# A hand-ordered attention and soft-MoE kernel: the last 64 rows' scores in float32r, two transfers fewer a pair of heads, four shared PSUM banks, and a new order of all operations

## The chip, the cores and the metric

The kernel runs on one core of a Trainium2 chip. The metric is the device time of one execution in microseconds (us); lower is better. Three executions of the kernel before took 482.61, 485.45 and 488.31 us, so its median is 485.45 us. The execution whose profile is read below took 482.46 us.

## The reference

Attention over 8 batches, 8 heads, 576 positions and head width 64, in float32, mixed with a read from a memory matrix; the result is rearranged to 4608 tokens of width 512 and goes through a soft mixture of 8 experts with 4 slots each.

```python
scores = scale * np.matmul(q, k.transpose(0, 1, 3, 2))
causal = np.triu(np.ones((S, S), dtype=bool), k=1)
scores = np.where(causal, -1000000000.0, scores)
...
local = np.matmul(a, v)
q_p = phi(q)
mem_ret = np.einsum('bhsd,bhde->bhse', q_p, M_prev)
mem_norm = np.einsum('bhsd,bhd->bhs', q_p, z_prev)[..., None] + 1e-06
...
return (g * mem_out + (1 - g) * local).astype(np.float32)
...
logits = x @ phi
...
slot_input = d.T @ x
...
    h = np.maximum(slot_input[e] @ w1[e], 0.0)
    slot_out[e] = h @ w2[e]
...
return (c @ slot_out).astype(np.float32)
```

## The kernel before

The 64 (batch, head) problems are handled as 32 pairs of heads, `n` = 0 to 31; the two heads of a pair share the 128 partitions. Each pair goes through the same list of small operations, each a Python function `op_<name>` of a few instructions:

- **Loads**, all issued by SyncE's queue (SP): `loadq` (L380, both the transposed q and three 128-column blocks in which the two heads' 64 rows stand block-diagonally), `loadk` (L385), `loadv` (L390, two transfers, one for each half of the partitions, into one buffer `vt` that all pairs share) and `loadm` (L395, memory matrix and norm).
- **Scores.** The 576 query rows are cut into rows 128 to 511 (`s.q1`, `s.q2`, `s.q3`) and the ends: rows 0 to 63 (`s.a`), 64 to 127 (`s.b`) and 512 to 575 (`s.z` for keys 0 to 511, `s.zb` for the last 64). `s.q*` multiplies in float32r (L437): q and k are split into a rounded high part and a remainder, `X[:, 0]`, `X[:, 1]` (by `qhi`, L359/L357, and `qlo`, L404) and `K2[:, 0]`, `K2[:, 1]` (by `kn`, `kl`, L410), and three products of the parts are added up, each over 64 partitions for each head. The ends go through `quads` (L415): float32 products in four column groups of 32. A float32 product of this kind stands in the trace as two instructions.
- **Softmax.** `max.*` on VectorE (DVE, L466) masks, scales, leaves PSUM and finds the maximum; `exp.*` on ScalarE (ACT, L474); `t.*` transposes the probabilities on TensorE (PE, L564) and `te.*` (ACT L354 or DVE L357) takes them out of PSUM.
- **Output.** `av.*` and `memb` (L415) multiply by v; `mema` (L415) multiplies the feature map of q by the memory. Two rows of factors travel through DRAM to be broadcast over partitions: the memory's norm (`nrw` L544 writes it, `nrr` L550 reads it back into `rb`, and `qn` L554 multiplies `qp` by it ahead of `mema`) and the softmax sums (`rt`, `rte`, then `rrw` L495 to L497 writes them in four transfers, `rrr` L501 reads them back into `rr`, and `xe.0` L635 and `mo` L628 multiply by them).
- **The soft MoE's statistics** (`x1` to `x5`) run over each finished block of 512 tokens, between the pairs' operations; after the last pair comes a closing part (`y*`), and then the experts (L934, L951) and the combination (L1008).

The order is written out by hand. `SEQ` lists 2546 operations such as `t.2@0:1` (operation, pair, and after the colon the PSUM bank); the operations are emitted in that order and `pin()` keeps every engine's instructions in it, the queue of SP's transfers too. A second table, `EV`, says for each movable operation which engine does it: `a` ACT, `v` DVE, `p` POOL (GpSimd). The weights of the experts are loaded meanwhile by 44 operations `w@x` in the same list (512 KB each).

PSUM's banks are three of `psT`, used in turn by transposes, norms, memory products and the MoE's pieces; one of `psO` for the running output `oa`; and two double ones of `psS` for scores.

Of the kernel before, what the change touches and what calls it, by code (L numbers as in the profile page):

```python
# [51 lines left out]
t.4@0:1 exp.q3h1@1 neps@1 rrw@0 max.q3h0@1 t.3@0:2 nmk@1 exp.q2h0@1 t.5@0:0 max.q2h1@1 exp.q3h0@1 s.q1@1:1 te.5@0 w@1
s.z@1 kn@2 exp.q2h1@1 max.zb@1 nred@1 te.3@0 te.4@0 t.0@1:0 nrw@1 exp.a@1 qhi@2 t.1@1:2 loadq@3 exp.b@1 max.q1h1@1
kl@2 t.2@1:1 max.z@1 exp.q1h1@1 av.0@0 rrr@0 qn@0 exp.z@1 max.q1h0@1 s.a@2:0 s.zb@2 av.2@0 max.zb@2 exp.q1h0@1 te.0@1
av.1@0 te.2@1 nrr@1 max.a@2 qlo@2 av.6@0 mema@0:10 te.1@1 loadk@3 rec@1 memb@0 av.3@0 qmin@2 loadm@2 s.b@2 loadv@1
rt@1:2 max.b@2 rte@1 s.q1@2:1 rrw@1 s.q2@2 max.q1h1@2 qexp@2 xe.0@0 s.z@2 mo@0 exp.a@2 exp.q1h1@2 xe.1@0 t.3@1:2
t.4@1:0 max.q2h0@2 te.3@1 x3.0@0:1 max.q2h1@2 te.4@1 t.5@1:2 qphi@2 x3e.0@0 s.q3@2:0 te.5@1 max.z@2 rrr@1 norm@2:0
kn@3 qn@1 av.0@1 exp.z@2 qhi@3 neps@2 exp.q2h1@2 mema@1:21 max.q1h0@2 qlo@3 nmk@2 exp.b@2 nred@2 exp.q1h0@2 s.b@3:1
kl@3 loadm@3 s.a@3 max.q3h1@2 av.3@1 exp.q2h0@2 nrw@2 av.6@1 memb@1 s.zb@3 max.q3h0@2 av.1@1 loadk@4 qmin@3 loadq@4
max.b@3 exp.q3h0@2 max.a@3 s.q2@3 exp.q3h1@2 s.q3@3:0 max.q2h1@3 qexp@3 xe.0@1 t.1@2:0 rec@2 nrr@2 t.3@2:1 te.1@2  # L60
max.q2h0@3 av.2@1 te.3@2 qphi@3 exp.q2h1@3 rt@2:0 loadv@2 t.5@2:1 max.zb@3 max.q3h1@3 rte@2 exp.q2h0@3 s.q1@3:1 rrw@2
max.q3h0@3 norm@3:0 te.5@2 max.q1h0@3 s.z@3 exp.q3h1@3 mo@1 s.zb@4:0 s.a@4 w@2 exp.q3h0@3 neps@3 t.4@2:1 xe.1@1 nmk@3
t.0@2:0 qhi@4 te.4@2 max.q1h1@3 x3.1@0:2 max.zb@4 qlo@4 te.0@2 max.a@4 nred@3 t.2@2:1 kn@4 t.0@3:0 x3e.1@0 nrw@3
exp.a@4 s.b@4 rrr@2 te.2@2 qn@2 av.0@2 exp.b@3 max.z@3 exp.a@3 mema@2:12 loadq@5 exp.q1h1@3 kl@4 exp.q1h0@3 av.3@2
qmin@4 loadm@4 exp.z@3 memb@2 av.6@2 loadk@5 s.q2@4 te.0@3 nrr@3 rec@3 s.q1@4:1 max.q2h1@4 rt@3:0 max.q2h0@4 av.2@2
rte@3 qexp@4 rrw@3 max.b@4 av.1@2 exp.b@4 exp.q2h1@4 xe.0@2 s.q3@4:0 mo@2 loadv@3 t.4@3:0 xe.1@2 qhi@5 t.3@3:2 te.4@3
max.q3h0@4 t.1@3:1 te.3@3 kn@5 max.q3h1@4 t.5@3:0 te.1@3 t.2@3:2 qphi@4 te.5@3 rrr@3 s.z@4 qn@3 te.2@3 exp.q3h1@4
norm@4:1 max.q1h1@4 s.zb@5:0 mema@3:20 neps@4 exp.q3h0@4 qlo@5 nmk@4 max.q1h0@4 kl@5 s.a@5 s.b@5 loadm@5 qmin@5
max.z@4 av.0@3 loadk@6 qexp@5 max.a@5 av.6@3 av.2@3 exp.z@4 qphi@5 memb@3 av.3@3 exp.q2h0@4 nred@4 av.1@3 exp.q1h0@4
max.b@5 nrw@4 exp.q1h1@4 loadq@6 mo@3 s.q3@5:1 loadv@4 xe.1@3 s.q2@5 w@3 norm@5:1 xe.0@3 x1.0@0:2 rec@4 neps@5  # L70
max.q3h1@5 x1.1@0 nmk@5 rt@4:0 x1l@0 nrr@4 t.3@4:1 max.q2h1@5 rte@4 t.0@4:2 max.q2h0@5 te.3@4 t.5@4:0 max.zb@5 exp.a@5
max.q3h0@5 rrw@4 t.4@4:1 te.0@4 x1m@0 te.5@4 s.q1@5:0 s.z@5 te.4@4 qhi@6 max.q1h1@5 kn@6 qlo@6 s.b@6:1 nred@5 x1e@0
loadk@7 av.0@4 max.z@5 nrw@5 kl@6 exp.q3h1@5 t.2@4:2 max.q1h0@5 t.1@4:0 te.2@4 x2@0:1 rrr@4 qn@4 exp.z@5 s.q3@6:0
x2m@0 exp.q1h1@5 s.q2@6 x2a@0 exp.q2h0@5 te.1@4 memb@4:2 mema@4:1 nrr@5 exp.q3h0@5 max.q3h0@6 exp.b@5 av.3@4 max.b@6
av.2@4 exp.q1h0@5 max.q3h1@6 loadm@6 loadq@7 s.zb@6 exp.q2h1@5 av.6@4 av.1@4 max.zb@6 max.q2h0@6 x2e@0 qmin@6 rec@5
s.z@6:0 loadv@5 qexp@6 xe.0@4 exp.q3h1@6 t.2@5:0 mo@4 t.4@5:2 te.2@5 xe.1@4 s.q1@6 te.4@5 qphi@6 rt@5:0 t.3@5:1 rte@5
# [1037 lines left out]
```

## Time and profile before

| | |
|---|---|
| runs of the kernel before | 482.61, 485.45, 488.31 us |
| profiled execution | 482.46 us, of which span 480.7 us |
| attention, 12 to 400 us of the span | PE 372.54 us busy of 388.00 |
| after 400 us (closing part, experts, combination) | 80.7 us |

The profile is read by engine: an engine is busy when an instruction runs on it, its idle time is put down to what ended it, and lines as L415 are those of the listing above. A helper's line stands for several operations: L415 is every float32 product in column groups, L437 every float32r score, L564 the transposes of probabilities. "PEld" is the loading of the stationary operand, which can run beside a product. All transfers of the pairs are issued on one queue, SP's, and run on 16 DMA engines.

### The profile page before, as it was taken

Reading aid. Unit: us, or ns where it says so; the run is one execution under the profiler, and the core shown is the slowest. Engines: PE = TensorE matmul, PEld = TensorE weight load, DVE = VectorE, ACT = ScalarE, POOL = GpSimd, SP = SyncE. Lnnn points to the kernel's source line nnn. Section 1 sums busy time; section 2 is a strip of 40 time slices with the busy share of each in tenths; the row PEclk is TensorE's granted clock in tenths of the full one; section 3 lists DMA queues with packets and bytes.
Section 4 is the critical chain, followed back from the end, with each engine's and each line's share of the span. In section 5 each row is a group of like instructions: output and inputs, shape, how many; then the busy total and the mean of one; then the engine's idle time right before and its main releaser. Section 6 shows DMA issues by size and latency. Waiting matters only on the chain.

```text
span 480.7 us, 16135 instructions
## 1 busy us (share of the span) xinstructions
PE 445.5 (93%) x6082; PEld 280.2 (58%) x6082; DVE 371.6 (77%) x1301; ACT 349.2 (73%) x1007; POOL 122.2 (25%) x139
## 2 busy tenths in 40 slices
...
GB/s 218 213 145 170 192 187 192 136 208 135 212 196 141 176 217 215 216 226 180 199 227 203 175 139 161 161 181 188 191 215 189 222 213 326 298 415 408 134 338 334
DMA packets 66300, 102.03 MB, mean 212 GB/s; under 512 B 11248, under 2 KB 41520, under 8 KB 66224
## 3 DMA queue, kind: packets, MB, share of 16 engines
...
## 4 chain that ended last, share of the span: by engine, by line
PE 46%; DMA 25%; DVE 15%; ACT 5%; SPq 4%; issue 3%; POOL 0%; DVEq 0%; ACTq 0%; POOLq 0%
PE oa L415 9%; DMA rm<-rs 9%; PE psT L564 8%; DMA rb<-rd 6%; PE psS L415 6%; DMA qq<-in_q_dram 5%; PE psS L437 5%; PE psT L415 4%; PE pf L934 3%; PE pc L1008 3%; DVE q L466 3%; DMA w<-in_w_dram 3%; DVE zq L466 2%; ACT w L354 2%; PE pf L951 2%
## 5 line engine op out<-in xcount | busy, mean ns | idle before, releaser
L354 ACT COPY at<-psT 128x512 f32<-128x512 f32 (+1 forms) x210 | 90.7, 481 | 30.8 <-PE psT L564 23.9
L474 ACT ACTIVATE q<-q,nm 128x384 f32<-128x384 f32 (+2 forms) x160 | 97.6, 613 | 5.5 <-DVE nm L466 5.4
L415 PE MATMUL oa<-at,mv 128*32 128x448 f32 (+4 forms) x1280 | 99.3, 423 | 1.1 <-DMA mv<-in_v_dram 1.0
L466 DVE CUSTOM_DVE_ANT_0 q<-psS,mv 128x512 f32<-128x512 f32 (+1 forms) x128 | 76.5, 613 | 6.2 <-PE psS L437 4.9
L564 PE MATMUL psT<-cs,q 128*128 128x128 f32 x480 | 74.0, 280 | 5.4 <-DVE xt L636 2.4
L474 ACT ACTIVATE zq<-zq,nm 128x256 f32<-128x256 f32 (+2 forms) x128 | 67.9, 533 | 8.7 <-DVE nm L466 8.5
L437 PE MATMUL psS<-K,X 64*128 64x512 f32 (+2 forms) x576 | 68.1, 358 | 1.6 <-DVE nm L466 1.6
L564 PEld LDWEIGHTS psT<-cs,q 128*128 128x128 f32 x480 | 53.9, 141 | 21.3 <-issue 5.8
L415 PE MATMUL psS<-k,qq 128*32 128x64 f32 (+2 forms) x1280 | 59.9, 298 | 1.3 <-DVE nm L466 1.2
L437 PEld LDWEIGHTS psS<-K,X 64*128 64x128 f32 x576 | 44.9, 184 | 17.0 <-issue 8.4
L564 PE MATMUL psT<-cs,zq 128*128 128x128 f32 x288 | 47.4, 278 | 2.3 <-DVE xt L636 0.9
L415 PEld LDWEIGHTS oa<-at,mv 128*32 128x32 f32 x1280 | 34.2, 110 | 25.1 <-issue 15.2
L415 PEld LDWEIGHTS psS<-k,qq 128*32 128x32 f32 x1280 | 33.4, 110 | 25.7 <-issue 9.6
L509 POOL TENSOR_SCALAR qp<-qq 128x576 f32<-128x576 f32 x15 | 24.9, 1658 | 61.5 <-PE psT L415 48.4
L415 PE MATMUL psT<-qp,q 128*32 128x64 f32 (+1 forms) x512 | 37.2, 407 | 2.3 <-DVE qp L554 1.8
L410 POOL TENSOR_TENSOR K<-k,K 128x512 fp32r<-128x512 f32 x28 | 36.9, 1317 | 7.1 <-ACT K L354 6.6
L564 PEld LDWEIGHTS psT<-cs,zq 128*128 128x128 f32 x288 | 32.9, 141 | 7.7 <-issue 1.5
L466 DVE CUSTOM_DVE_ANT_0 zq<-psS,mv 128x256 f32<-128x256 f32 x64 | 26.4, 419 | 12.4 <-PE psS L415 10.5
L415 PEld LDWEIGHTS psT<-qp,q 128*32 128x32 f32 x512 | 15.4, 109 | 27.3 <-issue 20.4
L474 ACT ACTIVATION_READ_ACCUMULATOR q<-q,nm 128x1 f32 x160 | 31.0, 194 | 0.0
L404 POOL TENSOR_TENSOR X<-qq,X 128x384 fp32r<-128x384 f32 x24 | 25.0, 1043 | 22.1 <-DVE X L357 12.2
L534 POOL TENSOR_TENSOR rn<-rn,rm 128x144 f32<-128x144 f32 x22 | 10.8, 491 | 75.4 <-DVE rn L529 35.8
...
## 6 DMA issues: line engine op xcount, KB each, us to landing
...
```

Source lines behind the costliest of these rows:

```text
L354: nc.scalar.copy(o, i)
L404: ALU_ENG[ev("qlo", n)].tensor_tensor(out=X[:, 1, 0:384], in0=st[n]["q"][:, 128:512], in1=X[:, 0, 0:384].bitcast(F32), op=ALU.subtract)
L410: ALU_ENG[ev("kl", n)].tensor_tensor(out=K2[:, 1, :], in0=st[n]["k"][:, 0:512], in1=K2[:, 0, :].bitcast(F32), op=ALU.subtract)
L415: nc.tensor.matmul(o[32 * g:32 * g + 32], w[:, 32 * g:32 * g + 32], x(g), start=start, stop=stop)
L437: nc.tensor.matmul(ps[:, c0:c0 + N], X[ROW[h], x, 128 * i - 128:128 * i], K2[ROW[h], y, 0:N], start=(x, y) == (0, 0), stop=(x, y) == (0, 1))
L466: nc.vector.tensor_tensor_reduce(out=sm, in0=src, in1=msk, op0=ALU.add, op1=ALU.min, scale=-0.125, scalar=m0, accum_out=acc_o)
L474: nc.scalar.activation(sm, sm, AF.Exp, scale=-1.0, bias=s["nm"][:, J:J + 1], accum_out=s["sum"][:, J:J + 1])
L509: ALU_ENG[ev("qmin", n)].tensor_scalar(out=st[n]["qp"], in0=st[n]["q"], scalar1=0.0, scalar2=None, op0=ALU.min)
L534: ALU_ENG[ev("nmk", n)].tensor_tensor(out=rn, in0=rn, in1=maskn.rearrange("a (u o) -> a u o", o=1).broadcast_to([128, 16, 9]), op=ALU.mult)
L564: nc.tensor.transpose(out=ps[:, 128 * x:128 * x + 128], in_=src[:, k0:k0 + 128], identity=ident)
L934: nc.tensor.matmul(ps[32 * g:32 * g + 32, :], si[:, c, 32 * (4 * eg + g):32 * (4 * eg + g) + 32], wt[0, eg, f, c // 2, g][:, c % 2, :], st ...
L1008: nc.tensor.matmul(ps[:, v2], (cst4[u][0:96, t4, :] if t4 < 8 else cst8[0:96, u, :]), so[0:96, dh], start=True, stop=True)
```

## The change

1. **`s.z` in float32r.** The block-diagonal copy of rows 512 to 575 now stands in `X` too, behind rows 128 to 511, and `s.z` becomes three products over the full 128 by 128 array for each of its two stretches of 256 keys (six instructions), where there were four column groups, twice two instructions each (sixteen). `X` grows from 384 used columns to 576, and so `qhi` and `qlo`. `s.zb` stays.
2. **Transfers.** `loadv` becomes one transfer of 128 partitions by 768 numbers (384 KB), with its zeros in it; it was two of 64 by 640 (160 KB each), and two memsets at the start. `rrw` writes its first six rows in one transfer, not two. A pair issues twelve transfers instead of fourteen.
3. **PSUM.** `psO` goes, and `oa` takes its bank from `psT`, which has four now.
4. **`qn`** may now run on POOL: in `EV` 23 pairs do it there and 9 on DVE; all 32 did it on DVE.
5. **The order.** `SEQ`, `EV` and `WORD` (which buffers late weights take) are written anew throughout.

```diff
-EV.update(qphi="v", qn="v")
+EV.update(qphi="v")
...
-        nc.gpsimd.memset(vt[64:128, 0], 0.0)
-        nc.gpsimd.memset(vt[0:64, 5], 0.0)
...
-    psO = tc.alloc_tile_pool(name="psO", bufs=1, space=PSUM)
...
-    X = spl.tile([128, 2, 512], F32R, name="X")
+    X = spl.tile([128, 2, S], F32R, name="X")
...
     def op_loadq(n):
         b, p = divmod(n, NP)
-        st[n]["q"] = qq[:, n % 2, 384:]
-        st[n]["qd"] = qq[:, n % 2, 0:384].rearrange("a (i x) -> a i x", i=3)
+        t = qq[:, n % 2]
+        st[n]["q"], st[n]["qx"], st[n]["qd"] = t[:, 256:832], t[:, 384:960], (t[:, 0:128], t[:, 128:256], t[:, 832:960])
...
     def op_loadv(n):
         b, p = divmod(n, NP)
-        for h in range(2):
-            nc.sync.dma_start(out=vt[ROW[h], h:h + 5], in_=v[b, p, ROW[h]])
+        nc.sync.dma_start(out=vt, in_=v[b, p])
...
     def op_qhi(n):
-        ENG[ev("qhi", n)](X[:, 0, 0:384], st[n]["q"][:, 128:512])
+        ENG[ev("qhi", n)](X[:, 0], st[n]["qx"])
 
     def op_qlo(n):
-        ALU_ENG[ev("qlo", n)].tensor_tensor(out=X[:, 1, 0:384], in0=st[n]["q"][:, 128:512], in1=X[:, 0, 0:384].bitcast(F32), op=ALU.subtract)
+        ALU_ENG[ev("qlo", n)].tensor_tensor(out=X[:, 1], in0=st[n]["qx"], in1=X[:, 0].bitcast(F32), op=ALU.subtract)
...
             for x0, x1 in zip(cuts, cuts[1:]):
-                quads(ps[:, c + x0 - k0:c + x1 - k0], s["qd"][:, i], lambda g: s["k"][:, x0:x1])
+                o = ps[:, c + x0 - k0:c + x1 - k0]
+                if t == "z":
+                    for x, y in ((0, 0), (1, 0), (0, 1)):
+                        nc.tensor.matmul(o, X[:, x, 448:576], K2[:, y, x0:x1], start=(x, y) == (0, 0), stop=(x, y) == (0, 1))
+                else:
+                    quads(o, s["qd"][i], lambda g: s["k"][:, x0:x1])
...
-        for h in range(2):
-            nc.sync.dma_start(out=rd[h, 128:512].rearrange("(i x) -> i x", i=3), in_=rts[3 * h:3 * h + 3])
+        nc.sync.dma_start(out=rd[:, 128:512].rearrange("h (i x) -> h i x", i=3), in_=rts[0:6])
...
-            st[n]["oa"], st[n]["parts"] = psO.tile([128, 512], F32, name="oa"), 0
+            st[n]["oa"], st[n]["parts"] = bank(), 0
```

The host side lays out q and v to match. As a sample of the order, the stretch behind `xe.1@13` in the list before and after (the part of pair 14's transposes up to its memory product):

```
before: xe.1@13 t.1@14:2 t.5@14:0 qmin@15 te.1@14 max.zb@15 qhi@16 loadm@15 t.2@14:1 te.5@14 loadk@17 t.0@14:2 te.2@14 exp.b@15
        t.3@14:0 te.0@14 max.q1h1@15 qlo@16 x3.0@3:1 te.3@14 t.4@14:2 qn@14 x3e.0@3 kl@16 s.b@16:1 max.z@15 te.4@14 rrr@14 s.a@16
        s.zb@16 mema@14:10
after:  xe.1@13 te.2@14 loadk@17 t.4@14:2 exp.q3h1@15 kn@16 xe.0@13 rrw@14 t.3@14:1 max.q2h1@15 te.4@14 t.1@14:3 kl@16 max.q2h0@15
        t.0@14:0 te.1@14 max.q1h0@15 x4.1@2:2 te.0@14 exp.b@15 s.b@16:0 qn@14 exp.a@15 s.a@16 x4a.1@2 norm@15:3 exp.q2h1@15 s.zb@16
        neps@15 t.5@14:0 te.3@14 max.z@15 x3.0@3:2 qhi@16 te.5@14 nmk@15 rrr@14 mema@14:13
```

More of the change, by code (lines that the diff above doesn't have):

```diff
@@ L52 @@
[L52 to L76, printed above, removed]
@@ new lines @@
+exp.q3h0@5 av.0@4:3 max.q1h1@5 max.q2h0@5 qhi@6 exp.b@5 av.1@4 max.q1h0@5 kn@6 max.z@5 exp.q1h0@5 rrr@4 memb@4:2
+s.zb@6:0 qlo@6 exp.q2h0@5 s.a@6 kl@6 mema@4:0 exp.q2h1@5 x2m@0 loadq@7 nmk@5 s.b@6 exp.q1h1@5 qmin@6 max.b@6 s.q3@6:1
+exp.a@5 nred@5 exp.z@5 max.a@6 av.6@4 nrw@5 av.2@4 max.q3h0@6 av.3@4 max.q3h1@6 exp.q3h0@6 loadv@5 s.q2@6 mo@4 qexp@6
+s.q1@6:1 rec@5 x2a@0 s.z@6 exp.a@6 xe.1@4 t.2@5:3 qhi@7 xe.0@4 nrr@5 t.3@5:1 max.q1h0@6 te.2@5 kn@7 rt@5:0 t.0@5:2
+te.3@5 rte@5 qlo@7 max.q2h0@6 t.5@5:3 loadm@6 te.0@5 max.q2h1@6 t.4@5:0 rrw@5 te.5@5 kl@7 t.1@5:1 qphi@6 x2e@0
@@ new lines @@
+max.q2h1@8 x3.1@1:0 max.z@8 t.2@7:3 x3e.1@1 qlo@9 t.0@7:1 max.q1h0@8 loadk@10 t.5@7:0 qphi@8 te.0@7 qn@7 s.q3@9:1
+te.3@7 max.q1h1@8 te.5@7 exp.z@8 s.q2@9:0 exp.q2h1@8 norm@8:1 rrr@7 s.zb@9 mema@7:02 neps@8 exp.q3h1@8 max.zb@9 nmk@8
+max.q3h1@9 exp.b@8 av.0@7:1 w@4 te.2@7 qmin@9 loadq@10 nred@8 s.b@9 exp.q2h0@8 memb@7 av.1@7 max.q3h0@9 nrw@8 qexp@9
+loadm@9 max.b@9 s.a@9 av.3@7 exp.q1h0@8 qphi@9 av.6@7 av.2@7 exp.a@8 exp.q1h1@8 mo@7 loadv@8 s.q1@9:1 exp.q3h1@9
+loadk@11 t.0@8:3 rec@8 loadq@11 t.5@8:1 xe.1@7 te.0@8 s.z@9 te.5@8 max.a@9 max.q2h1@9 t.3@8:3 qhi@10 xe.0@7 nrr@8
@@ new lines @@
+rt@8:0 t.4@8:1 kn@10 qlo@10 rte@8 te.3@8 t.2@8:2 max.z@9 t.1@8:0 te.2@8 rrw@8 kl@10 max.q2h0@9 x1.0@1:3 te.4@8
+max.q1h0@9 te.1@8 x1.1@1 norm@9:2 x1l@1 av.0@8:1 x1m@1 neps@9 exp.q3h0@9 max.q1h1@9 s.b@10:0 nmk@9 s.a@10 av.3@8
+exp.q2h1@9 av.6@8 qn@8 s.q3@10:1 x1e@1 rrr@8 exp.q1h0@9 s.q2@10 max.q3h0@10 exp.q2h0@9 x2@1:0 nred@9 mema@8:23 exp.b@9
+max.q3h1@10 exp.q1h1@9 nrw@9 exp.z@9 av.2@8 max.b@10 qmin@10 x2m@1 s.zb@10 av.1@8 exp.a@9 max.q2h1@10 x2a@1 rec@9
+memb@8 exp.q2h1@10 x4.0@1:0 xe.0@8 qexp@10 s.q1@10:1 mo@8 nrr@9 s.z@10 xe.1@8 x3.2@1:3 x4a.0@1 kn@11 qhi@11 t.5@9:1
@@ new lines @@
+av.6@11 av.3@11 max.q3h0@13 nmk@12 s.zb@13:0 s.a@13 exp.q1h0@12 loadv@12 mema@11:3 max.a@13 nred@12 exp.a@12
+exp.q2h1@12 mo@11 loadm@13 s.q2@13 qmin@13 nrw@12 xe.1@11 s.q1@13:1 qexp@13 s.z@13 max.q2h0@13 exp.q3h0@13 rec@12
+t.4@12:2 kn@14 xe.0@11 exp.a@13 t.0@12:0 qphi@13 rt@12:3 kl@14 x1.0@2:1 rte@12 max.zb@13 te.0@12 rrw@12 qhi@14 s.b@13
+te.4@12 max.q1h0@13 x1.1@2 qlo@14 norm@13:3 max.q2h1@13 x1l@2 t.5@12:0 neps@13 loadk@15 x1m@2 t.3@12:2 nmk@13 nrr@12
+te.5@12 max.b@13 t.2@12:1 te.3@12 x1e@2 t.1@12:3 max.z@13 te.2@12 x3.3@2:0 loadq@15 x2@2:2 x1d@1 rrr@12 x2a@2
```

415 lines of the change are left out of this document (212 added, 203 removed).

## The prediction, made before the changed kernel was run

> **What bounds the kernel now.** I read the shares of the engines first, then a table of two stages, then the chain of waits, then PE's order of time.
>
> ```profile
> PE 445.5 (93%) x6082; PEld 280.2 (58%) x6082; DVE 371.6 (77%) x1301; ACT 349.2 (73%) x1007; POOL 122.2 (25%) x139
> 12.00:400.00 388.00, 372.54 (x5327) 238.14 (x5321) 328.45 (x1195) 313.79 (x937) 117.63 (x128) 1.00 0.67 189
> PE 46%; DMA 25%; DVE 15%; ACT 5%; SPq 4%; issue 3%; POOL 0%; DVEq 0%; ACTq 0%; POOLq 0%
> 6.93 0.87 PE psS L415 x24
> ...
> L639 DVE TENSOR_TENSOR xt<-xt,psT x60: 207/416/686, 30.0 to 404.6; 128x448 f32<-128x448 f32 x8, 128x64 f32<-128x64 f32 x8, 128x384 f32<-128x384 f32 x8, 128x128 f32<-128x128 f32 x8
> ```
>
> The second row is the stage that the change rewrites, 12 to 400 us of the span: PE is busy in 372.5 of 388 us at full granted clock (1.00), DVE in 328 (85%), ACT in 314 (81%), POOL in 118 (30%), the DMA engines at 0.67. PE sets the pace and idles only 15.5 us. The chain (third row) still runs 25% through transfers: they are just in time, so a shorter distance between issue and use shows. Attention's first score starts at 6.93 and its last sum at 404.6: 398 us for 32 pairs, 12.4 each. So what counts is, first, how much PE work the new list holds, and second, how much of it turns into waiting.
>
> **The change, part by part.**
>
> *PE, `s.z`.* The rows below are from PE's order of time: start, length, count. The start of the next row less the start of a row is what it really took.
>
> ```profile
> 213.12 1.07 PE L415 MATMUL psS<-k,qq 128*32 128x256 f32 x16
> 214.01 1.06 PE L648 MATMUL psT<-xt,rm 128*32 128x128 f32 x32
> ...
> 225.24 1.07 PE L415 MATMUL psS<-k,qq 128*32 128x256 f32 x16
> 226.24 0.33 PE L736 MATMUL psT<-cs,rm 128*128 128x128 f32 x1
> 226.41 0.60 PE L564 MATMUL psT<-cs,q 128*128 128x128 f32 x4
> 226.84 0.60 PE L564 MATMUL psT<-cs,zq 128*128 128x128 f32 x4
> ...
> 455.64:456.36 0.72, 0.72 (x8) 0.72 (x7) 1.00 0.99 321
> ...
> 444.00:451.20 7.20, 5.45 (x33) 0.53 0.17 68
> ...
> 449.62 2.71 PE L1008 MATMUL pc<-k,w 96*128 96x256 f32 x13
> ...
> L564 PEld LDWEIGHTS psT<-cs,q 128*128 128x128 f32 x480 | 53.9, 141 | 21.3 <-issue 5.8 <-ACT q L474 3.1 <-ACT at L354 1.8
> ```
>
> The old `s.z` (sixteen instructions) takes 0.89 us when column groups follow (213.12 to 214.01). The new one is six float32r products of 256 columns. The nearest row is the combination L1008, the same but with 96 instead of 128 rows: the window 455.64 to 456.36, at clock 1.00, holds six steps between starts (it counts one product at each edge too) in 0.72 us, 0.12 each. At a clock of 0.53 (the two rows behind it) a step is 2.71 / 13 = 0.21, so the clock, not the row count, makes the price. I take 0.72 for six, and save 0.89 - 0.72 = 0.17 a pair, **5.4 us**. The ends: nothing if each step costs 0.15 us, and a loss of 0.66 us a pair if the load of the weights stops hiding (a rival below).
>
> The Trainium skill speaks against this step: *TensorE: Matmul & The Clock Gate*, "Packing small matmuls" ("The mechanism"), says that a weight load overlaps a running product only when the two use different row groups, and six products over all 128 rows share theirs. By that rule load and product would add up. The trace has the transposes L564, also over the full array, at 0.11 us a step with a load of 0.141 us each, so the rule does not hold strictly here.
>
> *PE, changes of shape.* The array works in three shapes here: full (128 columns: transposes, now `s.z`), column groups (128\*32) and two row halves (64\*128, `s.q*`).
>
> ```profile
> 203.15 0.61 PE L714 MATMUL psT<-cs,xt 128*128 128x128 f32 x4
> 203.68 0.64 PE L415 MATMUL oa<-at,mv 128*32 128x512 f32 x4
> ...
> 200.28 0.28 PE L485 MATMUL psT<-cs,r 128*9 128x128 f32 x1
> 200.40 0.27 PE L564 MATMUL psT<-cs,q 128*128 128x128 f32 x1
> ```
>
> Four transposes take 0.43 us when transposes follow (226.41 to 226.84) and 0.53 when column groups follow: leaving the full shape costs 0.10. The old `s.z` takes 0.89 when column groups follow and 1.00 when a transpose does: leaving column groups costs 0.11. I counted changes along both lists, PE's operations alone: leaving column groups 82 times before, 53 after; leaving the full shape 84 before, 44 after; leaving row halves 64 both times. That saves 29 x 0.11 + 40 x 0.10 = **7.2 us**. Most of it is the order: in 24 pairs `s.z` now stands between two full-array operations. Unknown is whether float32r next to float32 transposes in the full shape drains as well: 55 such borders, 0 to 0.10 us each, 0 to 5.5 us. One row says no drain: a 9-column transpose (L485) is followed after 0.12 us by L564, but both are float32. I take 1 us.
>
> *DVE, ACT, POOL.*
>
> ```profile
> L554 DVE TENSOR_TENSOR qp<-qp,rb 128x576 f32<-128x576 f32 x32 | 24.8, 774 | 3.8 <-DMA rb<-rd 3.8
> L410 POOL TENSOR_TENSOR K<-k,K 128x512 fp32r<-128x512 f32 x28 | 36.9, 1317 | 7.1 <-ACT K L354 6.6
> L404 POOL TENSOR_TENSOR X<-qq,X 128x384 fp32r<-128x384 f32 x24 | 25.0, 1043 | 22.1 <-DVE X L357 12.2 <-PE psT L564 8.7 <-POOL K L410 0.4
> L404 DVE TENSOR_TENSOR X<-qq,X 128x384 fp32r<-128x384 f32 x8 | 5.5, 683 | 0.0
> L359 POOL TENSOR_SCALAR X<-qq 128x384 fp32r<-128x384 f32 x26 | 14.4, 552 | 60.4 <-PE psS L437 12.7 <-PE psT L522 11.4 <-DVE qp L516 9.9
> L359 POOL TENSOR_SCALAR K<-k 128x512 fp32r<-128x512 f32 x17 | 10.5, 618 | 41.7 <-PE psS L437 26.9 <-PE psT L564 8.7 <-ACT qp L507 4.4
> ```
>
> `qn` leaves DVE in 23 pairs: -23 x 0.774 = -17.8 us. `qlo` with 576 columns for 384 takes about 0.95 on DVE and 1.45 on POOL (by the two POOL rows, 384 and 512 wide); DVE does 14, not 8: 13.3 - 5.5 = +7.8. It also gets six `nmk`, three `kl`, two `kn` and four `te` more, some +7. So DVE stays near 325 us, 86% of a stage of 377. ACT gives seven `kn`, four `qmin` and four `te` away, about -9. POOL gains 23 `qn` (1.45 each, 33 us) and the wider `qhi` (0.7) and `qlo`: from 118 to about 165 us, 44%. None becomes the bound by its sum.
>
> But `X` and `K2` exist once, and `s.z` reads them now. From the last product that reads them to the first of the next pair I count, in PE work, a median of 4.8 us before and 3.7 after; `qhi`, `qlo`, `kn`, `kl` in a row on POOL take 0.7 + 1.45 + 0.62 + 1.32 = 4.1. They are mostly shared among engines, and `kn` is rarely behind `qlo`. I take 0, with 0.4 us in half of the pairs, 6 us, as the far end.
>
> *Transfers.*
>
> ```profile
> L550 SPq DMA_DIRECT2D rb<-rd x64: 592/615/1813, 14.9 to 397.4; - x64
> DVE qp L554 <- DMA rb<-rd: 3.8, 5, 1.4
> DVE xt L635 <- DMA rm<-rs: 5.8, 6, 1.8
> DVE xt L628 <- DMA rm<-rs: 5.3, 5, 1.6
> 104.08 3.27 DMA rb<-rd
> ...
> 129.13 2.95 DMA rb<-rd
> ...
> 185.43 6.59 DMA rb<-rd
> ...
> 212.96 3.99 DMA rb<-rd
> ...
> 253.70 4.09 DMA rb<-rd
> ```
>
> SP issues 64 transfers fewer, which frees its queue and takes nothing off the end. The v transfers bring 64 KB more a pair, 2 MB of 102. What matters is the distance from issue to use, which I measured in PE work along the lists: from `nrr` to `qn` a median of 5.8 us before and 4.3 after, from `rrr` to the first product with `rr` 5.3 and 4.2. The list's PE work before, 359 us by prices as above, took 398, so a listed microsecond lasts 1.11: 4.3 becomes 4.8. The second of `nrr`'s transfers is issued 0.6 later, so those over 4.2 us are late; the pieces of the chain above run from 2.95 to 6.59, one of five above that. Before, with 6.4 us of distance, DVE waited five times. I take a quarter of the pairs late by 1 us, 8 us; `qn` now waits on POOL, with `kn`, `qhi`, `qlo` behind it, and `mema` on PE behind that. About half comes out of slack that PE's other waits leave: **+4 us**. Ends: -1 (the waits stay as they are and SP's shorter queue helps) and +12 (all of it, and `rr`'s as well).
>
> *Banks.* With four shared banks the next writer stands less than 0.7 us of PE work behind the evacuation in 126 of 419 uses, before in 186 of 388. I take -1 us (0 to -3).
>
> *Start, experts and combination* keep their operations: 0.
>
> **Sum.** -5.4 - 7.2 + 1 + 4 - 1 = -8.6 us, from 482.46 to 473.9 for an execution like the profiled one. That one lies 3.0 us under the median of the three runs shown (485.45) and under all of them; I put the median of the changed kernel slightly above the sum, at **474.5**.
>
> **Rivals.** *A: the waits eat it.* Both shortened distances (transfers 4.3 for 5.8, `X` and `K2` 3.7 for 4.8) take their far ends, 12 + 6 us for the 4 that I took, or about two thirds of that: 480 to 486. For it: the DMA share of the chain, and PE work that ends sooner needs the same transfers sooner. Against: PE idles only 15.5 us in the stage before, and a wait at one place gives slack to the next.
>
> *B: slower, the load of the weights shows.*
>
> If full-array float32r products do not hide their loads, a step is 0.141 + 0.12 = 0.26 us, six are 1.56, and `s.z` loses 0.67 a pair, 21 us, for the 5.4 gained: 482.46 - 8.6 + 5.4 + 21 = 500. It decides from a step of (0.89 + 7.2 / 32) / 6 = 0.19 us on. Against: the steps of L1008 at full clock. It is what the skill's rule above would give.
>
> *C: more gain.* The new list also clears half of the 15.5 us that PE idles, by its banks and by the tasks moved off ACT: 464 to 469.
>
> **How the numbers follow.** My forecast (469 to 479) gets 0.52, A 0.26, B 0.08, C 0.12, anything else 0.02. The range 466 to 485 leaves out B, the lower half of C and the top of A, some 0.18. Changes under 1% of 485.45 (480.6 to 490.3) are about what a measurement of this kernel cannot tell from none. Faster by more: forecast, C and a quarter of A, 0.70; within 1%: the rest of A, 0.19; slower: B and the unnamed, 0.11.
>
> **What would show it.** Right: L437 has six more rows of 128\*128 a pair with starts 0.12 us apart; `s.z` is left 0.7 us after it starts when a transpose follows; PE's busy time in the attention stage falls by about 12 us while its idle time there grows by no more than 5; attention's last L639 comes near 396. Wrong: steps of 0.2 us and more in `s.z` (B); PE or POOL waiting for `rb<-rd` for tens of microseconds, or `psS` waiting for `X` and `K` on POOL (A). If PE's busy time does not fall, my count of shape changes was worth nothing. And if DVE passes 90% of the stage it has become the bound.

## The result and the profile after

| | median of 20 runs | lowest to highest |
|---|---|---|
| kernel before, beside it | 485.23 us | 481.74 to 489.65 |
| changed kernel | 482.72 us | 479.16 to 490.34 |

The ratio is 0.9949, with a 95% interval of 0.9924 to 0.9974: 2.5 us faster, where 11 were forecast for the median and 8.6 by the forecast's sum. Ratios, here and below, leave out runs in which the chip was disturbed, the medians do not; where the two differ, the ratio counts. The profiled execution of the changed kernel took 482.45 us with a span of 480.7 us, the same span as the profiled one of before. The two profiles are of equally long executions: the one of before lies 2.8 us under its median, the one of the changed kernel at it. They show what was exchanged for what, and not the 2.5 us.

The shares of the engines, then the window of the attention stage (PE, PEld, DVE, ACT, POOL busy; clock; DMA share; GB/s), then the chain that ended last, all of the changed kernel:

```profile
PE 431.5 (90%) x5762; PEld 288.1 (60%) x5762; DVE 378.3 (79%) x1289; ACT 341.2 (71%) x1001; POOL 168.8 (35%) x155
```

```profile
12.00:400.00 388.00, 361.12 (x5020) 249.52 (x5022) 335.57 (x1185) 304.73 (x929) 165.61 (x148) 1.00 0.67 196
```

```profile
PE 32%; DMA 27%; DVE 21%; ACT 5%; POOL 5%; issue 4%; SPq 4%; DVEq 0%; POOLq 0%; ACTq 0%
DMA rb<-rd 10%; DMA rm<-rs 9%; PE psT L414 9%; DVE q L470 4%; PE psS L441 4%; PE psT L567 4%; PE pf L937 3%; DVE zq L470 3%; DMA rd<-rq 3%; DVE qp L519 2%; DVE at L357 2%; PE pc L1011 2%; ACT w L354 2%; POOL qp L557 2%; PE pf L954 2%
```

PE is busy 11.4 us less in the stage (372.54 to 361.12), at the same clock, and it idles 11.4 us more (15.5 to 26.9). In the chain, PE's share falls from 46% to 32%; transfers (25% to 27%; the two reads `rb` and `rm` alone 15% to 19%), DVE (15% to 21%) and POOL (0 to 5%) take its place. The work went away and waiting stands where it was. The chain of before, by its lines:

```profile
PE oa L415 9%; DMA rm<-rs 9%; PE psT L564 8%; DMA rb<-rd 6%; PE psS L415 6%; DMA qq<-in_q_dram 5%; PE psS L437 5%; PE psT L415 4%; PE pf L934 3%; PE pc L1008 3%; DVE q L466 3%; DMA w<-in_w_dram 3%; DVE zq L466 2%; ACT w L354 2%; PE pf L951 2%
```

The attention stage ends no earlier (the last sum, L642, starts at 405.1; before, at 404.6):

```profile
L642 DVE TENSOR_TENSOR xt<-xt,psT x60: 209/416/689, 26.9 to 405.1; 128x448 f32<-128x448 f32 x8, 128x64 f32<-128x64 f32 x8, 128x384 f32<-128x384 f32 x8, 128x128 f32<-128x128 f32 x8
```

First the new `s.z`, in PE's order of time (start, length, count) and as two groups (products and their loads: busy, mean ns of one, idle before):

```profile
61.76 0.60 PE L567 MATMUL psT<-cs,q 128*128 128x128 f32 x4
62.20 0.60 PE L567 MATMUL psT<-cs,zq 128*128 128x128 f32 x4
62.55 0.96 PE L433 MATMUL psS<-K,X 128*128 128x256 f32 x6
63.35 0.60 PE L567 MATMUL psT<-cs,q 128*128 128x128 f32 x4
```

```profile
L433 PE MATMUL psS<-K,X 128*128 128x256 f32 x192 | 31.0, 296 | 0.3 <-POOL X L403 0.3
L433 PEld LDWEIGHTS psS<-K,X 128*128 128x128 f32 x192 | 24.9, 189 | 1.6 <-POOL X L403 0.5 <-issue 0.2 <-DVE nm L470 0.2
```

From 62.55 to 63.35 it takes 0.80 us until the next transposes start. That is 0.09 more than six steps of 0.118, but no price of the border between float32r and float32: the four transposes ahead of it take 0.35 us (62.20 to 62.55) where four ahead of transposes take 0.44 (61.76 to 62.20), so `s.z` starts 0.09 sooner and its first step is longer by as much. Transposes and `s.z` together take 1.15 us, which is 0.44 and six steps. In the ten pairs where `s.z` has transposes on both sides the four and `s.z` take 1.15 to 1.21 us; by the medians the first step of `s.z` is 0.20 us and the other five are 0.12. Nothing waits for weights: each load takes 0.189 us and hides behind products 0.118 us apart.

Who waits for transfers and for `X` and `K2` now (engine, line, what it waited for: us in total, times, longest):

```profile
POOL qp L557 <- DMA rb<-rd: 39.0, 13, 5.8
POOL K L359 <- PE psS L433: 29.2, 9, 8.6
...
POOL X L359 <- PE psS L433: 15.3, 5, 6.0
...
DVE xt L631 <- DMA rm<-rs: 8.8, 5, 5.4
DVE qp L557 <- DMA rb<-rd: 6.2, 4, 2.0
...
DVE xt L638 <- DMA rm<-rs: 5.3, 6, 1.9
...
SPq L504 <- DMA rs<-rts: 23.9, 21, 3.0
SPq L553 <- DMA rd<-rq: 21.8, 14, 3.1
...
PEld psS L441 <- POOL K L409: 2.8, 8, 0.7
...
PEld psS L441 <- POOL X L403: 2.2, 4, 1.1
...
PEld psS L441 <- DVE X L403: 1.9, 3, 0.9
```

The same queue's and PEld's rows of the kernel before:

```profile
SPq L550 <- DMA rd<-rq: 10.8, 11, 2.6
...
SPq L501 <- DMA rs<-rts: 8.7, 8, 2.0
...
PEld psS L437 <- POOL X L404: 0.7, 1, 0.7
```

The reader is to see three things. The product by `rb` stands on POOL and on DVE for 45 us where DVE alone stood 3.8; how much of this holds up anything else these rows do not say, and 1 and 2 below measure it. SP, which issues the reads `nrr` and `rrr`, now stands for the writes that precede them for 45.7 us where it stood 19.5: both hops of each round trip, not the last alone, have lost their slack. And PE's loads for scores wait for the float32r parts of `q` and `k` for 6.9 us in these rows, where one row had 0.7.

A stretch of the chain in the changed kernel (start, length, what; dots stand for pieces left out) shows a round trip closing on itself:

```profile
262.82 3.10 DMA rb<-rd
...
266.06 1.43 POOL qp L557
267.49 1.34 issue
268.82 0.69 ACT qp L510
269.52 0.02 issue
269.54 0.69 ACT qp L515
...
275.53 0.29 DVE rn L532
...
275.85 0.98 DVE rn L537
276.83 0.02 issue
276.85 0.43 DVE rq L541
...
277.55 4.68 DMA rd<-rq
...
282.94 4.27 DMA rb<-rd
```

The read of `rb` for pair 20 lands, POOL multiplies, ACT fills the buffer of `qp` for pair 22, whose features, norm and reduction follow, and with them its write (4.68 us) and its read (4.27). From read to read the ring of two pairs took 20.1 us here, with 7.8 us of landings in it (3.10 and 4.68), on the chain that ended last; on this stretch a landing that is late by a microsecond lengthens it by as much.

Two tables of my own from the records of both executions. The first is landing times, from a transfer's issue to the last of its completions; medians over the pairs, first issue to last landing where a step has several transfers:

```
                            before   changed
write of rd (nrw)             3.46      3.15
read of rb (nrr)              4.45      4.41
write of rs (rrw)             3.14      3.34
read of rm (rrr)              5.05      4.75
read of rb issued behind the landing of its write   0.68   0.07
```

The landings are what they were, and the order now leaves nothing between them: the read goes out at most 0.07 us behind its write's landing in half of the pairs.

The second is where PE starts late. For each operation of the list I took the time from its first product to that of the next, less its price by the rows (with 0.11 or 0.10 for a change of shape and 0.09 for leaving `s.z`), and summed what exceeds 0.15 us, by the operation that started late:

```
                    scores  transposes  rt   norm  memory  av   other  all
before                4.3      11.4     0     2.3    3.5   1.9   2.5   25.8
changed              12.0       7.0     5.7   4.4    6.7   3.6   2.7   42.1
```

By the same prices the list holds 363.3 us of PE work before and 353.6 after. The 353.6 counts 0.09 us for leaving `s.z` in 28 pairs, 2.5 us that the rows above show to be won back at its start.

### The profile page after: what moved, and what is told of

Same layout as the page of the kernel before. It is cut to its first block, busy times and chain, and to the rows that moved or that the text cites. A ratio compares the mean times of both kernels' runs of the same rounds, so it can differ in the third digit from the quotient of the medians.

```text
span 480.7 us, 15438 instructions
## 1 busy us (share of the span) xinstructions
PE 431.5 (90%) x5762; PEld 288.1 (60%) x5762; DVE 378.3 (79%) x1289; ACT 341.2 (71%) x1001; POOL 168.8 (35%) x155
## 2 busy tenths in 40 slices
DMA packets 65658, 104.09 MB, mean 217 GB/s; under 512 B 10608, under 2 KB 40880, under 8 KB 65584
## 4 chain that ended last, share of the span: by engine, by line
PE 32%; DMA 27%; DVE 21%; ACT 5%; POOL 5%; issue 4%; SPq 4%; DVEq 0%; POOLq 0%; ACTq 0%
DMA rb<-rd 10%; DMA rm<-rs 9%; PE psT L414 9%; DVE q L470 4%; PE psS L441 4%; PE psT L567 4%; PE pf L937 3%; DVE zq L470 3%; DMA rd<-rq 3%; DVE qp L519 2%; DVE at L357 2%; PE pc L1011 2%; ACT w L354 2%; POOL qp L557 2%; PE pf L954 2%
## 5 line engine op out<-in xcount | busy, mean ns | idle before, releaser
L414 PE MATMUL psT<-at,mv 128*32 128x64 f32 (+4 forms) x1536 | 103.4, 389 | 2.3 <-DMA mv<-in_v_dram 2.1
L354 ACT COPY at<-psT 128x256 f32<-128x256 f32 (+1 forms) x209 | 87.3, 481 | 23.9 <-PE psT L567 21.4
L441 PE MATMUL psS<-K,X 64*128 64x512 f32 (+2 forms) x576 | 72.3, 364 | 5.0 <-DVE nm L470 2.6
L414 PEld LDWEIGHTS psT<-at,mv 128*32 128x32 f32 x1536 | 40.4, 110 | 32.6 <-issue 20.6
L557 POOL TENSOR_TENSOR qp<-qp,rb 128x576 f32<-128x576 f32 x23 | 33.5, 1458 | 53.1 <-DMA rb<-rd 39.0
L512 POOL TENSOR_SCALAR qp<-qq 128x576 f32<-128x576 f32 x19 | 31.8, 1672 | 42.6 <-PE psT L414 41.2
L631 DVE TENSOR_TENSOR xt<-psT,rm 128x448 f32<-128x448 f32 (+7 forms) x60 | 23.6, 432 | 12.9 <-DMA rm<-rs 8.8
L414 PEld LDWEIGHTS psT<-qp,q 128*32 128x32 f32 x512 | 15.0, 109 | 31.0 <-issue 19.5
L357 DVE COPY at<-psT 128x512 f32<-128x512 f32 (+1 forms) x52 | 29.4, 585 | 4.6 <-PE psT L567 1.9
L359 POOL TENSOR_SCALAR K<-k 128x512 fp32r<-128x512 f32 x22 | 14.9, 675 | 50.6 <-PE psS L433 29.2
L519 DVE SCALAR_TENSOR_TENSOR qp<-qq,qp 128x576 f32<-128x576 f32 x32 | 31.1, 973 | 0.3 <-ACT qp L515 0.2
```

The lines of the kernel that those rows point to most:

```text
L354: nc.scalar.copy(o, i)
L357: nc.vector.tensor_copy(out=o, in_=i)
L414: nc.tensor.matmul(o[32 * g:32 * g + 32], w[:, 32 * g:32 * g + 32], x(g), start=start, stop=stop)
L441: nc.tensor.matmul(ps[:, c0:c0 + N], X[ROW[h], x, 128 * i - 128:128 * i], K2[ROW[h], y, 0:N], start=(x, y) == (0, 0), stop=(x, y) == (0, 1))
L512: ALU_ENG[ev("qmin", n)].tensor_scalar(out=st[n]["qp"], in0=st[n]["q"], scalar1=0.0, scalar2=None, op0=ALU.min)
L519: ALU_ENG[ev("qphi", n)].scalar_tensor_tensor(out=t, in0=st[n]["q"], scalar=0.0, in1=t, op0=ALU.max, op1=ALU.add)
```

## The experiments

All were timed in five rounds against the kernel before. "a" is a variant of the changed kernel, "b" of the one before. The two kernels themselves stand at 482.72 (0.9949) and 485.23.

**1, 2. What the waits on both reads cost.** The products by `rb` and `rm` take a constant block of `cs` instead; all transfers are still issued.

```diff
-        ALU_ENG[ev("qn", n)].tensor_tensor(out=s["qp"], in0=s["qp"], in1=s["rb"], op=ALU.mult)
+        x, f = fixed(s["qp"])
+        ALU_ENG[ev("qn", n)].tensor_tensor(out=x, in0=x, in1=f, op=ALU.mult)
```

The factor `f` is `cs[:, 0:64]`, repeated; `xe.0` and `mo` take it likewise.

> The changed kernel, but qn, xe.0 and mo multiply by a constant block of cs instead of the factors that come back through DRAM; both round trips are still issued and land, and nobody waits for them. Theory T (late broadcasts eat the saved PE work): about 10 us faster than the changed kernel, near 472, PE's idle time in 12 to 400 us falls from 27 to about 12. Rival X (X and K2, each there once, are refilled too late): less than 3 us faster, the waits on POOL X and K stay. Rival P (PE's work itself is dearer than counted): no change.

> The same edit in the kernel before. Theory T: the old list had 1 to 1.5 us more distance, so it gains less, 2 to 5 us (near 481). If it gains as much as the changed kernel does, late broadcasts are no difference between the two and T falls.

473.19 us (ratio 0.9744, 0.9687 to 0.98) and 481.55 (0.9935, 0.9895 to 0.9975). The waits cost 9.5 us in the changed kernel and 3.7 in the one before (9.9 and 3.2 by the ratios, each to some 3 or 2 us either way). Without them the change is worth 8.4 us by the medians, 9.3 by the ratios (0.9744 / 0.9935 = 0.981): two thirds to three quarters of the 12.6 us that the forecast has without its term for transfers. PE's idle time fell by less than expected of 1: in 12 to 390 us from 23.6 to 19.5 us, where 27 to 12 in 12 to 400 us were expected.

**3, 4. The new `s.z` alone.** In 3 the changed kernel computes `s.z` by column groups again, in 4 the kernel before computes it in float32r. In both, steps that prepare later pairs had to move behind `s.z`: twelve loads of k and q in 3, 44 of `qhi`, `qlo`, `kn`, `kl` in 4. In 3 `X` also has 384 used columns again, so `qhi` and `qlo` are shorter.

```diff
-                if t == "z":
-                    for x, y in ((0, 0), (1, 0), (0, 1)):
-                        nc.tensor.matmul(o, X[:, x, 448:576], K2[:, y, x0:x1], start=(x, y) == (0, 0), stop=(x, y) == (0, 1))
-                else:
+                if True:
                     quads(o, s["qd"][i], lambda g: s["k"][:, x0:x1])
```

> The changed kernel with s.z in column groups again (X with 384 used columns; twelve loads of k and q moved behind s.z). PE's work by the list grows by 8 to 10 us. Theory T (PE has waits to fill): less than half of it shows, 1 to 4 us slower than the changed kernel, near 485. Rival P (PE work counts in full): 8 to 10 us slower, near 491.

> The kernel before with s.z in float32r alone, its list kept except that 44 steps qhi, qlo, kn, kl are moved behind the s.z that reads what they overwrite. PE saves about 2 to 5 us. PE work alone: 3 us faster than before. Rival X (refilling X and K2 is what costs): slower than before by 5 us or more, with PE waiting for X and K.

487.24 (1.0007, 0.9964 to 1.005) and 511.12 (1.0533, 1.0487 to 1.0578). In its own order the float32r `s.z` is worth 4.5 us by the medians and 2.8 by the ratios, whose intervals overlap; in the old order, with 44 steps moved, it loses 26. 4 is no measure of `s.z`: it moves much else. But it shows that the step needs an order of its own, since `X` and `K2` are refilled only behind it.

**5, 6. Each read alone.** The edits of 1, one at a time: only `qn` (5), only `xe.0` and `mo` (6).

> The changed kernel with only qn freed from its factors (a constant block in their place; the round trip still runs). Theory T: the two round trips cost about 9.5 us together; PE's stalls ahead of mema add up to 7 us and those behind late row sums (ahead of rt, and one of 3.5 us near the end) to 10, so this alone gives 3 to 6 us, near 478. If it gives nothing, the wait of qn is covered by the other one.

> The changed kernel with only xe.0 and mo freed (a constant block in place of the row sums' factors). Theory T: 4 to 7 us faster, near 477; the stalls ahead of rt go, those ahead of mema stay.

481.21 (0.9927, 0.9886 to 0.9968) and 483.84 (0.9914, 0.9863 to 0.9965): by the ratios 1 and 2 us better than the changed kernel, where both together give 9.9; each is within the noise of no gain. Both expectations were missed. With `rb` free the late starts ahead of `rt`, which hangs on `rm`, grow from 5.7 to 9.2 us; with `rm` free those ahead of the memory product from 6.7 to 8.6. So either wait seems to cover the other.

**7. Later uses.** Only the list changes: `qn`, `mema`, `xe.0` and `mo` move back to the distances of before (`nrr` to `qn` from 4.3 to 5.5 us of listed PE work, `rrr` to first use from 4.2 to 5.3). A sample:

```diff
-s.b@16:0 qn@14 exp.a@15 s.a@16 x4a.1@2 norm@15:3 exp.q2h1@15 s.zb@16 neps@15 t.5@14:0 te.3@14 max.z@15 x3.0@3:2 qhi@16
-te.5@14 nmk@15 rrr@14 mema@14:13
+s.b@16:0 exp.a@15 s.a@16 x4a.1@2 norm@15:3 exp.q2h1@15 s.zb@16 neps@15 t.5@14:0 qn@14 te.3@14 max.z@15 x3.0@3:2 qhi@16
+te.5@14 nmk@15 rrr@14 exp.z@15 qlo@16 exp.q1h1@15 s.q2@16 mema@14:13
```

> The changed kernel's list with qn, mema, xe.0 and mo moved later within it where that is possible, until the distance from issue to use is 5.3 us of PE work (median of nrr to qn 4.3 before the move, 5.5 after; of rrr to first use 4.2 and 5.3). Nothing is left out. Theory T: half or more of the 9.5 us comes back, near 477. If moving them later only moves the wait (mema nearer to what needs it), no change: 482 to 483.

486.82 (1.0081, 1.004 to 1.0123): 4 us slower by the medians, 6 by the ratios, missed. Late starts of PE add up to 42.0 us as before the edit (42.1). A later use gives the landing more time and takes it from whatever comes next.

**8. Large loads behind the reads.** 42 loads of k, q, v and weights move behind the next `nrr` or `rrr`, so that the reads find less in flight.

```diff
-nrr@14 s.q2@15
+nrr@14 w@11 s.q2@15
```

> The changed kernel's list with 42 large loads (weights, k, q, v) that stood less than 2.5 us of PE work ahead of an nrr or rrr moved right behind it. Theory T with the landing times of the trace (3.4 us with less than 0.3 MB in flight, 4.8 us with more than 1 MB): broadcasts land some 0.4 us sooner, 2 to 4 us faster, near 480. If landing times do not depend on what is ahead in the queue, no change.

499.49 (1.0304, 1.0248 to 1.0361): 17 us slower. SP issues in order, and the loads now stand behind reads that themselves wait there for their writes (SP's waits in this kernel):

```profile
SPq L552 <- DMA rd<-rq: 37.1, 20, 5.3
SPq L503 <- DMA rs<-rts: 34.0, 27, 2.9
```

71 us of standing on the two, for 45.7 in the changed kernel: a load behind it is late by the wait of another step. The reads themselves did land sooner, as expected (a single transfer of `rb` in 3.34 us by the median for 3.73, of `rm` in 3.62 for 4.07), and it did not help.

**9, 10, 11. Is it the order of the ring?** 9 puts `rec` of the next pair ahead of this pair's products by `rm` and `rt` earlier. 10 cuts `qn` in two, one half each on DVE and POOL. 11 does both.

```diff
-mo@11 loadm@13 s.q2@13 qmin@13 nrw@12 xe.1@11 s.q1@13:1 qexp@13 s.z@13 max.q2h0@13 exp.q3h0@13 rec@12 t.4@12:2 kn@14
-xe.0@11 exp.a@13 t.0@12:0 qphi@13 rt@12:3
+rec@12 mo@11 loadm@13 s.q2@13 qmin@13 nrw@12 xe.1@11 s.q1@13:1 rt@12:0 qexp@13 s.z@13 rte@12 max.q2h0@13 exp.q3h0@13
+rrw@12 t.4@12:2 kn@14 xe.0@11
```

```diff
-        ALU_ENG[ev("qn", n)].tensor_tensor(out=s["qp"], in0=s["qp"], in1=s["rb"], op=ALU.mult)
+        for e, x0, x1 in ((nc.vector, 0, 320), (nc.gpsimd, 320, 576)) if ev("qn", n) == "p" else ((nc.vector, 0, 576),):
+            e.tensor_tensor(out=s["qp"][:, x0:x1], in0=s["qp"][:, x0:x1], in1=s["rb"][:, x0:x1], op=ALU.mult)
```

> The changed kernel; in the list of the order, the reciprocal of the next pair's row sums is put ahead of this pair's first product by the landed rm in 17 pairs (or right behind the last exponential it needs), and in 25 pairs its transposition, the copy and the write to memory come earlier with it, by 0.6 us of PE work on average. Nothing is left out. Theory of loops (the round trip of rm is chained from pair to pair: landing, product on DVE, next reciprocal behind it, next transposition, next write, next read, about one period of 12 us): the stalls of PE ahead of that transposition, 5.7 us in the changed kernel, fall below 2 us, and since the loop of rb is left, the time falls only by 1 to 3 us against the changed kernel (480 to 482). Rival, DVE with 336 of 388 us busy sets the period whatever the order of these: stalls move to other places and the time stays within 1 us of the changed kernel's.

> The changed kernel with the product of the 23 pairs that POOL multiplies by rb cut in two: 320 columns on DVE, 256 on POOL, so that the step takes about 0.7 us instead of 1.46 behind the landing, for about 0.45 us more of DVE in each of 23 pairs (10 us in all). Nothing is left out. Theory of loops: the loop of rb gets 0.7 us shorter and that of rm is left: the stalls ahead of the memory products fall from 6.9 us to 4 or less, the time by 0 to 2 us against the changed kernel. Rival, DVE sets the period: it has 10 us more to do and the time is 2 to 6 us above the changed kernel's.

> Both edits of the two runs before in one kernel. Theory of loops: both loops are shorter, and the gain is more than the sum of the two alone: 3 to 6 us below the changed kernel, 477 to 480. Rival, DVE sets the period: no better than the worse of the two.

486.21 (0.9921, 0.9861 to 0.9981; the ratio is the changed kernel's within the noise), 487.73 (1.0022, 0.9976 to 1.0068) and 489.54 (1.008, 1.0036 to 1.0124). My theory of how the loop closes found no support: in 9 the late starts ahead of `rt`, which were to fall below 2 us, only go from 5.7 to 5.0, in a profiled execution that is itself long (489.95 us), and the time says neither yes nor no. In 10 a shorter step made the time 3.5 us (ratio) to 5 us longer, as the rival said, and 11 is slower still. DVE's waits in 10:

```profile
DVE qp L558 <- DMA rb<-rd: 13.7, 13, 2.1
...
DVE xt L632 <- DMA rm<-rs: 8.3, 5, 4.9
DVE xt L639 <- DMA rm<-rs: 7.4, 8, 2.7
```

DVE stands for `rb` 13.7 us, for 6.2 in the changed kernel: half of `qn` brought its wait along to an engine that much else queues on. That this wait, and not the 10 us of added work, made it slower is argued from 12 and not shown.

**12, 13. Is it DVE's work?** The addition of the memory's part is done on 16 columns only.

```diff
-            for o, c0, c1 in xpieces(n):
-                nc.vector.tensor_tensor(out=o, in0=o, in1=st[n]["om"][:, c0:c1], op=ALU.add)
+            for o, c0, c1 in xpieces(n)[:1]:
+                nc.vector.tensor_tensor(out=o[:, 0:16], in0=o[:, 0:16], in1=st[n]["om"][:, c0:c0 + 16], op=ALU.add)
```

> The changed kernel with the last addition of each pair on DVE (the memory's part onto the output, up to 512 columns) done on 16 columns only, so the output lacks the rest of that part; every wait, transfer, bank and the order stay. It takes about 18 us of work off DVE (60 additions of 0.4 us to some 30 of 0.07). Theory DVE (in the changed kernel the vector engine, 336 of 388 us busy and waiting in order for landings for 20 us more, has no room left for the landings' lateness: its waits for score products fell from some 21 us before to 5): the time falls by 5 to 10 us against the changed kernel, and the waits for rb and rm fall with it. Theory landings (the round trips alone set the period): 0 to 2 us.

> The same edit in the kernel before: the same part of the output is left out. Theory DVE: there the vector engine waits for PE's scores for 21 us, so taking 18 us of work off it gains little, 0 to 3 us against the kernel before. If it gains as much as in the changed kernel, the vector engine's work is no part of what the change ran into.

481.21 (0.9965, 0.9926 to 1.0004) and 481.36 (0.9938, 0.9899 to 0.9977). With DVE busy 16 us less (319.43 for 335.57 of 388), the changed kernel gains nothing beyond the noise; the kernel before gains 3 us. In the changed kernel DVE's stock of work is not the bound; a wait in its queue is another matter (10).

**14, 15. Shorter landings.** Both reads bring a quarter of their bytes or less, and the products use what was read over again; the order stays. The bytes of all transfers fall with it, from 104.09 to 89.67 MB in 14.

```diff
-            nc.sync.dma_start(out=rr[ROW[h]], in_=st[n]["rs"][h].rearrange("(o x) -> o x", o=1).broadcast_to([64, S]))
+            nc.sync.dma_start(out=rr[ROW[h]][:, 0:128], in_=st[n]["rs"][h][0:128].rearrange("(o x) -> o x", o=1).broadcast_to([64, 128]))
...
-            src = st[n]["rd"][:, h, :].rearrange("g (o x) -> o g x", o=1).broadcast_to([64, 4, 144])
+            src = st[n]["rd"][0:1, h, :].rearrange("g (o x) -> o g x", o=1).broadcast_to([64, 1, 144])
```

> The changed kernel with both broadcast reads cut: that of rb brings 144 columns in place of 576 and that of rm 128, each used again for the other columns, so the products by them have wrong factors there. Every issue, wait, write to memory and product stays, in the same order; only the landing should come earlier than the 4.41 and 4.75 us (first issue to last landing, medians) of the changed kernel. Theory landings: per pair the period follows the landings, and the time falls by some 5 us or more if each lands a us earlier, as far toward the 9.5 us of the kernel without these waits as the landings shrink. Rival, the waits' price comes from their place in the order and not from the landing's length: within 2 us of the changed kernel.

> The same edit in the kernel before. Theory landings: there the uses stand 1.3 us of PE work further behind the issues, so shorter landings gain less than half of what they gain in the changed kernel, at most the 3.7 us that freeing the waits gained. Rival: the same in both.

467.09 (0.9634, 0.9585 to 0.9683) and 471.44 (0.974, 0.9688 to 0.9792). By my reckoning of landings, in the changed kernel `rb` lands in 3.41 us (4.41) and `rm` in 3.73 (4.75), and the small writes come sooner too (2.62 for 3.15, 3.03 for 3.34). The time falls by 15.6 us, and that of the kernel before by 2.6%, 12.6 us. That is not under half of the other, as was expected, and both expectations took the gains of 1 and 2 for the limit, which both runs passed. A read that lands sooner cannot by itself save more than all the waits for it, and these are worth 9.5 and 3.7 us. So the rest, some 6 and 9 us, is something else that the smaller reads bring. The records show what it can be: the loads land sooner as well (medians from issue to landing, of `rb` and `rm` from the first issue to the last landing):

```
                       load q  load k  write rd  read rb  read rm
before                   5.14    4.31      3.46     4.45     5.05
2, waits freed           5.11    4.23      3.39     4.25     5.09
15, small reads          4.25    3.80      2.65     3.47     4.06
17, half                 5.35    4.12      3.44     3.93     4.16
changed                  4.44    4.30      3.15     4.41     4.75
14, small reads          4.26    3.80      2.62     3.41     3.73
16, half                 4.46    4.25      3.03     4.08     4.08
```

And where 2 frees the waits for the reads, waits for loads come forward, which 15 does not have (2, then 15):

```profile
POOL X L359 <- DMA qq<-in_q_dram: 25.9, 6, 9.7
```

```profile
POOL X L359 <- DMA qq<-in_q_dram: 4.8, 2, 3.5
```

So transfers as a whole hold back the kernel before as well, and not the landings of the two reads alone. No run took the parts of this further gain apart. The two chains (changed kernel's variant, then the other's):

```profile
PE 43%; DVE 25%; DMA 14%; issue 5%; ACT 4%; POOL 3%; SPq 3%; DVEq 0%; POOLq 0%; ACTq 0%
```

```profile
PE 74%; DVE 12%; ACT 5%; issue 4%; DMA 2%; POOL 1%; SPq 1%; POOLq 0%; DVEq 0%; ACTq 0%
```

In the variant of before PE now carries 74% of the chain: there the old list is mostly bound by PE. In the changed one DVE and DMA still have 39%, and PE's late starts ahead of scores stay (13.2 us, for 3.6).

**16, 17. A version that computes everything.** The factors travel as float16: half of the bytes.

```diff
-        rd = st[n]["rs"] = drm.tile([2, S], F32, name="rs")
+        rd = st[n]["rs"] = drm.tile([2, S], F16, name="rs")
...
-        nc.vector.reciprocal(out=rq, in_=rq)
+            nc.vector.reciprocal(out=rh, in_=rq)
...
-        rb = st[n]["rb"] = atp.tile([128, S], F32, name="rb")
+        rb = st[n]["rb"] = atp.tile([128, S], F16, name="rb")
```

`rts`, `rd` and `rr` become float16 in the same way.

> The changed kernel with the factors of both round trips kept as float16: the copy of the transposed reciprocals and the memory's reciprocals are written as float16, written to memory, broadcast and multiplied as such. All is computed; the factors are rounded to 11 bits. Each broadcast read brings half the bytes, every wait and the order stay. Theory landings: with a quarter of the bytes the landings were 1.0 us shorter and the time 15.6 us lower; with half of them some half of that, 4 to 9 us below the changed kernel. Rival, it was the changed shape of the read (fewer pieces a row) and not the bytes: within 2 us.

> The same in the kernel before. Theory landings, as the quarter reads showed it: the landings set the pace there too, and it gains some half of the 12 us of the quarter reads, 3 to 8 us. Rival: within 2 us of the kernel before.

478.15 (0.9888, 0.9836 to 0.994) and 480.77 (0.9938, 0.9906 to 0.997). With both reads landing in 4.08 us the changed kernel gains 4.6 us by the medians and 3.0 by the ratios, the one before 4.5 and 3.0, so each ends at the low edge of what was expected or just under it. Here the loads of q and k land as before (the table above), so this is nearer to what the two reads alone are worth than 14 is. The packets are as many as in the changed kernel, so the bytes have a part in it:

```profile
DMA packets 65658, 94.51 MB, mean 198 GB/s; under 512 B 27184, under 2 KB 44976, under 8 KB 65584
```

The changed kernel has 65658 packets as well, with 104.09 MB; 14 has 53370. The first of the two is the fastest here that computes everything, at the price of factors of 11 bits; its interval still overlaps the changed kernel's.

## Why the prediction was wrong, step by step

**The step that failed** is the term for transfers: "I take a quarter of the pairs late by 1 us, 8 us", half of it out of slack, "+4 us". Experiments 1 and 2 put it at 5.8 us by the medians (9.5 less 3.7), some 6.8 by the ratios, give or take some 3.5. The traces show what its working left out. I priced a wait as the tail of landings beyond the distance to the use, pair by pair. But the distance was also cut upstream, at the writes (SP's standing for them went from 19.5 to 45.7 us), the reads follow on each other from pair to pair, and a late one delays the next. And "PE sets the pace", from its 372.5 busy us of 388, was half true: lighter reads alone gain 12.6 us in the kernel before, with PE's work as it was. The 25% of transfers in its chain said so; I read them as "just in time" and used them for one term only.

That term is not the whole miss. Without the waits the change is worth 8.4 to 9.3 us for the 12.6 forecast, so 3 to 4 us are lost elsewhere; the next step is where I look for them. And 2.4 of the 11 us were never a gain of the change: the sum starts from a profiled execution 3.0 us under the median. From 485.45 it gives 476.9, not 474.5.

**`X` and `K2`** I took at 0, with 6 us as the far end. The late starts ahead of score products grew from 4.3 to 12.0 us. Waits for the two tiles are part of it (PEld's rows above: 6.9 us for 0.7), waits for the score banks another. They stay when the landings are shortened (13.2 and 3.6), so they do not come from the landings of the two reads. No run took them apart, and that they are the 3 to 4 us is not shown.

**PE's work** came as forecast: 363.3 to 353.6 us by the list, 11.4 of busy time for "about 12". `s.z` steps take 0.118 us (0.12 forecast); changes of shape in the trace fall by 69 (250 to 181), as counted. The unknown border costs nothing that shows, where I took 1 out of 0 to 5.5. The sign of **banks** was right: late starts ahead of transposes fall by 4.4 us, for the 1 taken, though the order changed with the banks and no run parts the two.

**DVE, ACT, POOL.** POOL's 165.6 us are the "about 165". DVE came to 335.6, not "near 325"; some of it is the same work taking longer (`qphi` 973 ns for 874, `qlo` 1.05 us for the 0.95 taken). Neither is a bound by its sum (12).

**The rivals.** A, "the waits eat it", was what happened, and 482.72 lies in its 480 to 486; I gave it 0.26. It lies in my whole range of 466 to 485 too, but only because that was drawn wide enough to hold most of A. Its sign in the trace was named: POOL waiting for `rb` for tens of microseconds (39.0). B fell: no weight load shows. The rule of the Trainium skill (*TensorE: Matmul & The Clock Gate*, "Packing small matmuls"), that loads overlap products only in other row groups, is not borne out by L433: loads of 0.189 us over the same rows fit into steps of 0.118. The same section of the Trainium skill also allows for a load into a background weight buffer; no run here shows whether that is what happens. C did not come. Of the signs that I gave for the forecast, busy time fell; idle time, which was to grow by at most 5, grew by 11.4, and the last sum came at 405.1, not near 396.

**What stays open:** which edges close the ring of the landings. Two guesses (9, 10) brought nothing, and moving the last hop (7) does not help. That transfers hold the changed kernel back is shown by 1, 14 and 16; how much of the 15.6 us of 14 is the two reads and how much is lighter traffic for all, and how the list should absorb it, is not.
